# First load of a one-core decode block cut to x and the biases; its query weights join the first keys

## The chip, the core and the metric

The kernel runs on one core of a Trainium2 chip. The metric is the device time of one execution in microseconds (us); the number for a kernel is the median of several executions. A profiled execution gives a trace: every instruction on TensorE (PE for matmuls, PEld for the weight loads ahead of them), VectorE (DVE), ScalarE (ACT), GpSimd (POOL) and SyncE (SP), and every packet of the 16 DMA engines.

## What is computed

One decode step for four tokens (B = 4, model width D = 448): a layer norm, attention with 16 query heads over 8 key/value heads of width 256 on the last 1024 positions of a cache, a residual, then a layer norm twice over and an MLP with a GELU and a second residual. Cut to what matters:

```python
W = min(4096, max(256, Sk // 4))              # 1024 of 4096 positions
q = (layernorm(x) @ wq)                       # 448 -> 16 heads x 256
scores = einsum("bhqd,bhkd->bhqk", q, k[last W]) * Dh ** -0.5
o = einsum("bhqk,bhkd->bhqd", softmax(scores), v[last W])
h = x + o @ wo                                # 4096 -> 448
y = layernorm(layernorm(h))
h2 = h + gelu(y @ w1 + b1) @ w2 + b2          # 448 -> 1792 -> 448
```

All data is float32. With four tokens nearly all of the traffic is weights, keys and values, each read once.

## The kernel before

The work goes by key/value head `g` from 0 to 7. For each head the kernel projects the queries (`project_q`, matmul L214, copy to `qs` L216, transposes L222, a reduction and two copies into `qT` L225 and L229), takes the scores (`scores`, matmul `s` L237, then the maximum and the exponential), transposes the probabilities (`transpose_p`, L262), multiplies by the values (`values`, matmul `po` L276), scales and transposes the result (`heads`) and adds it to the output projection (`project_o`, `acc` L311). Queries are projected two heads ahead of their values and one ahead of their scores.

All inputs of the heads are packed on the host into eleven wide arrays, `stream0` to `stream10`, by the table `LOADS`: entry 0 holds the query weights of head 0, the keys of head 0 and the query weights of head 1 (`[("q", 0, 0), *parts("k", 0), ("q", 1, 0)]`). Each is 128 rows (one per partition) and is loaded by one DMA on SP's queue into one of three slots of the pool `ring` (tile `t`, named `stream`). A load is issued when `part` is first asked for something in it, and SP holds back the issue until all readers of the slot's earlier contents are done. So the first three loads are issued at once, and the fourth only when the first slot is free: when head 0's keys and the second query weights have been used.

The first slot is filled by two DMAs. Array `first` (L98) has 128 rows of 1828 floats: the 1792 columns of head 0's query weights (`WC`), and behind them 36 columns (`X0`) with x transposed (16), the bias b1 (16) and the bias b2 (4). Array `stream0` (L100) then brings the keys of head 0 and the query weights of head 1, 9984 columns, into the same tile.

The order of TensorE's instructions is written out by hand: the order in the program text is the order on the engine. Other engines are ordered by the framework's scheduler. At the start TensorE takes the means of x and of its squares (L193 and L194, `column_mean`), POOL the power for the reciprocal root (L208), DVE writes the normed x into `yT` (L330 to L332). Then comes `project_q` of head 0, and behind it four plus two transposes that lay out the biases and x for the end of the kernel (`pb` L348 and L349, `px` L352 and L353, copied into `rs` by ACT L350 and DVE L354). Then come the scores of head 0 and `project_q` of head 1.

After the eighth head's scores the slots are reused for the last values (`v7`, L137), the last two output weights (L383), w1 (L386) and w2 (L390, four DMAs). `keep_warm` matmuls (L361) are filler without a use for the result, at fixed places in the last third. The end is the second layer of the MLP (`second`, matmul `py` L511), a copy (L522) and two output DMAs (L525).

Of the kernel before, what the change touches and what calls it, by code (L numbers as in the profile page):

```python
# [8 lines left out]
F32 = mybir.dt.float32  # L9
# [6 lines left out]
B, D = 4, 448  # L16
HQ, HKV, SK, DH = 16, 8, 4096, 256
# [3 lines left out]
P = 128  # L21
H = P // 2
ND = 4
# [7 lines left out]
WC = 4 * D  # L31
QU = KV // 4
X0 = 2 * ND * B + 4
LOW = 3 * P
# [3 lines left out]
def parts(kind, g, quarters=range(4)):  # L38
    return [(kind, g, i) for i in quarters]


LOADS = [
    [("q", 0, 0), *parts("k", 0), ("q", 1, 0)],
    [*parts("k", 1), ("q", 2, 0), *parts("v", 0, (0, 1))],
    [*parts("v", 0, (2, 3)), ("o", 0, 0), *parts("k", 2)],
    [("q", 3, 0), *parts("v", 1), ("o", 1, 0), *parts("k", 3, (0,))],
    [*parts("k", 3, (1, 2, 3)), ("q", 4, 0), *parts("v", 2, (0, 1, 2))],
    [*parts("v", 2, (3,)), ("o", 2, 0), *parts("k", 4), ("q", 5, 0)],
    [*parts("v", 3), ("o", 3, 0), *parts("k", 5, (0, 1))],
    [*parts("k", 5, (2, 3)), ("q", 6, 0), *parts("v", 4)],  # L50
# [6 lines left out]
def width(part):  # L57
    kind, g, _ = part
    if kind in "kv":
        return QU  # L60
    return WC + {("q", 0): X0, ("q", HKV - 1): -LOW // 2}.get((kind, g), 0)


SLOT = max(sum(map(width, parts)) for parts in LOADS)
W1C = 3 * F + F // 2
C = D // 4
# [5 lines left out]
def block_kernel(ctx: ExitStack, tc, first, streams, v7, wo67, w1, w2, wq_low, out):  # L72
    nc = tc.nc
# [3 lines left out]
    once = ctx.enter_context(tc.tile_pool(name="once", bufs=1))  # L77
# [8 lines left out]
    def slot(name):  # L86
        return ring.tile([P, SLOT], F32, tag="t", name=name)

    held = {}
    streams_first = streams[0]  # L90

    def part(kind, g, i=0):
        while (kind, g, i) not in held:
            src = streams.pop(0)
            t = slot("stream")
            wanted = LOADS[len(LOADS) - len(streams) - 1]
            if src is streams_first:
                nc.sync.dma_start(t[:, : WC + X0], first)  # L98
            at = WC + X0 if src is streams_first else 0
            nc.sync.dma_start(t[:, at : at + src.shape[-1]], src)  # L100
            at = 0
            for one in wanted:
                held[one] = t[:, at : at + width(one)]
                at += width(one)
            if ("q", HKV - 1, 0) in wanted:
                held["low"] = t[:H, at : at + LOW]
                for h in range(2):
                    nc.sync.dma_start(t[h * Q : (h + 1) * Q, at : at + LOW], wq_low[h, :, : Q // 8, :])
        return held[kind, g, i]

    def wq_parts(t):
        parts = [(a, a, slice(0, 512), t[:, a * 512 : (a + 1) * 512]) for a in range(3)]
        n = t.shape[-1] - 3 * 512
        low = 512 - 2 * n
        for i in range(2):
            parts.append((3, 3 + i, slice(low + i * n, low + (i + 1) * n), t[:, 3 * 512 :]))
        if low:
            parts.append((3, 3, slice(0, low), held["low"]))
        return parts
# [4 lines left out]
    def load_k(g, h, c):  # L124
        return part("k", g, 2 * h + c).rearrange("p (b k) -> p b k", b=B)
# [5 lines left out]
    def load_v(g, c):  # L131
        return part("v", g, c).rearrange("p (c b d) -> p c b d", c=2, b=B)
# [53 lines left out]
    def spread(t):  # L186
        return t[..., ::GAP]
# [23 lines left out]
    def project_q(g, parts):  # L211
        pq = ps_m.tile([P, 512], F32, tag="m", name=f"pq{g}")
        for j, a, cols, w in parts:
            nc.tensor.matmul(pq[j * Q : (j + 1) * Q, cols], yT[: w.shape[0], a, :], w, start=True, stop=True)  # L214
        qs = once.tile([P, 512], F32, tag="qs", name=f"qs{g}")
        nc.scalar.copy(qs, pq)  # L216

        pt = ps_m.tile([P, 512], F32, tag="m", name=f"pqt{g}")
        if g == HKV - 1:
            keep_warm(3, pt)  # L220
        for i in range(2 * REP):
            nc.tensor.transpose(pt[:, i * P : (i + 1) * P], qs[:, i * P : (i + 1) * P], ident)  # L222
        q = work.tile([P, 2 * REP, B], F32, tag="q", name=f"q{g}")
        quadrants = pt.rearrange("p (i j q) -> p i q j", i=2 * REP, j=4)
        nc.vector.tensor_reduce(q, quadrants[:, :, :B, :], axis=AX.X, op=ALU.add)  # L225

        src = q.rearrange("p (r c) b -> p c b r", r=REP)
        for i in range(2):
            nc.vector.tensor_copy(qT[g % 2][:, :, :, i * REP : (i + 1) * REP], src)  # L229

    def scores(g):
        s = [ps_s.tile([P, 512], F32, tag="s", name=f"s{g}_{h}") for h in range(2)]
        mx = work.tile([P, 2], F32, tag="mx", name=f"mx{g}")
        for h in range(2):
            for c in range(2):
                for b in range(B):
                    nc.tensor.matmul(  # L237
                        s[h][b * Q : (b + 1) * Q, :], qT[g % 2][:, c, b, :], load_k(g, h, c)[:, b, :],
                        start=(c == 0), stop=(c == 1),
                    )  # L240
            nc.vector.reduce_max(mx[:, h : h + 1], s[h], axis=AX.X)  # L241
        nm = work.tile([P, 1], F32, tag="nm", name=f"nm{g}")
        nc.vector.tensor_max(nm, mx[:, 0:1], mx[:, 1:2])
        nc.vector.tensor_scalar_mul(nm, nm, -SCALE)  # L244
        p = work.tile([P, 2 * 512], F32, tag="p", name=f"p{g}")
        sums = work.tile([P, 2], F32, tag="sums", name=f"sums{g}")
        for h in range(2):
            nc.scalar.activation(  # L248
                p[:, h * 512 : (h + 1) * 512], s[h], AF.Exp, bias=nm, scale=SCALE,
                accum_out=sums[:, h : h + 1],  # L250
            )
        rec = work.tile([P, 1], F32, tag="rec", name=f"rec{g}")
        nc.vector.tensor_add(rec, sums[:, 0:1], sums[:, 1:2])
        nc.vector.reciprocal(rec, rec)
        return p, rec
# [52 lines left out]
    def project_o(g, wt):  # L308
        for i in range(4):
# [6 lines left out]
            for j in range(4):  # L316
# [3 lines left out]
                )  # L320

    t0 = part("q", 0)
    xT = t0[:, WC : WC + ND * B].rearrange("p (a b) -> p a b", a=ND)
    d = work.tile([P, ND, B], F32, tag="d", name="d_x")
    centred(d, xT, "x")
    sx = work.tile([P, ND, B], F32, tag="sx", name="sx")
# [3 lines left out]
    nc.vector.tensor_mul(yT[:, :3, :B], d[:, :3, :], rx[:, None, :].to_broadcast([P, 3, B]))  # L330
    nc.vector.tensor_mul(yT[:H, 3, :B], d[:H, 3, :], rx[:H, :])
    nc.vector.tensor_mul(yT[H:, 4, :B], d[H:, 3, :], rx[H:, :])  # L332
    project_q(0, wq_parts(t0[:, :WC]))


    b1T = t0[:, WC + ND * B : WC + 2 * ND * B].rearrange("p (c j) -> p c j", c=4)
    b2T = t0[:, WC + 2 * ND * B : WC + X0]
    nc.vector.tensor_copy(spread(zT), xT)
    b1s = work.tile([P, 2 * 512], F32, tag="p", name="b1s")
    b2s = b1s[:, 4 * P : 5 * P]  # L340
# [11 lines left out]
    nc.tensor.transpose(px[:, :P], zT.rearrange("p j q -> p (j q)"), ident)  # L352
    nc.tensor.transpose(px[:, P : 2 * P], b2s, ident)  # L353
    nc.vector.tensor_copy(rs[:, : 2 * P], px[:, : 2 * P])  # L354

    tail = []

    def keep_warm(n, to=None):
        to = tail[0][:, 0, :] if to is None else to
        for _ in range(n):  # L360
            nc.tensor.matmul(to[:Q, :512], idle[:, :Q], idle, start=True, stop=True)  # L361


    p, rec = scores(0)
    project_q(1, wq_parts(part("q", 1)))
    transpose_p(0, p)
    for g in range(HKV):
        if g + 1 < HKV:
            p, rec_next = scores(g + 1)
# [9 lines left out]
        else:  # L379
# [8 lines left out]
            at = 0  # L388
# [96 lines left out]
    for i in range(2):  # L485
        for j in range(4):
            if i <= j:
                at = PAD + C * j - P * (j - 1 + i) if j else PAD
# [34 lines left out]
    for i, queue in ((1, nc.scalar), (0, nc.sync)):  # L523
        at = i * H + LIFT
# [72 lines left out]
```

## Time and profile before

| | us |
|---|---|
| median of 3 runs | 213.75 (213.74 to 213.86) |
| the profiled execution, its own time | 213.85 |
| its span, first to last instruction | 212.1 |
| TensorE matmuls busy in the span | 147.8 (70%) |
| DVE busy | 36.8 (17%) |
| ACT busy | 24.5 (12%) |
| POOL busy | 6.2 (3%) |
| SP's DMA queue (q1), share of the 16 DMA engines | 96.9% |

The span and the time around it differ by 1.8 us, which no row covers. Busy shares are averages over the whole span. What decides is which wait ends last in each stretch, and for that the chain of waits, the DMA share by stretch and the issue times on SP are read together.

### The profile page before, as it was taken

The numbers are of one execution on the slowest core, as the hardware profiler recorded it, in microseconds if no ns is written. First come the engines' busy times: TensorE is split into PE (matmuls) and PEld (weight loads), VectorE is DVE, ScalarE is ACT, GpSimd is POOL, SyncE is SP. The second block draws the span as 40 slices with busy tenths as digits, with TensorE's granted clock in tenths as the row PEclk, the third lists the DMA queues.
The fourth block names the chain that finished last, engine by engine and source line by source line (L and its number), as shares of the span: only waits on it lengthen the run. The fifth ranks groups of instructions, "written<-read, shape, count | busy, mean of one in ns | idle before, by whom it ended". The sixth has DMA issues, their size and how long they took to land.

```text
span 212.1 us, 2553 instructions
## 1 busy us (share of the span) xinstructions
PE 147.8 (70%) x1103; PEld 57.1 (27%) x1103; DVE 36.8 (17%) x152; ACT 24.5 (12%) x58; POOL 6.2 (3%) x20
## 2 busy tenths in 40 slices
PE   0469704972891883980795780687599999999994
PEld 0333301230120520230222220131124434335443
DVE  1521400320112110220113011031022023001330
ACT  2011300030002100030003000030003002100310
POOL 6200000000000000000000000000000000000110
PEclk9999985697579599698579799589679999999999
DMA  7999898999989999998999999999999999999991
GB/s 297 414 429 510 351 501 382 449 436 419 490 365 475 407 436 442 407 490 382 457 425 425 436 425 447 401 463 409 455 414 443 389 475 387 413 426 419 427 396 61
DMA packets 3146, 88.39 MB, mean 417 GB/s; under 512 B 368, under 2 KB 576, under 8 KB 960
## 3 DMA queue, kind: packets, MB, share of 16 engines
q1 hardware_dynamic: 3120, 88.24, 96.9%
q8 instruction: 8, 0.13, 0.2%
q14 instruction: 2, 0.02, 0.0%
q10 hardware_dynamic: 16, 0.00, 0.0%
HBM read 88.23 MB, written 0.01 MB: 416 GB/s over the span
## 4 chain that ended last, share of the span: by engine, by line
DMA 70%; PE 26%; DVE 1%; SPq 1%; issue 1%; ACT 0%; ACTq 0%
DMA stream<-stream 59%; DMA w<-w 11%; PE s L237 9%; PE po L276 6%; PE wait L361 3%; PE acc L311 3%; PE ppt L262 1%; PE pq L214 1%; PE pot L301 1%; DVE o L293 0%; PE tail L361 0%; PE py L511 0%; SPq L100 0%; ACT p L248 0%; SPq L390 0%
## 5 line engine op out<-in xcount | busy, mean ns | idle before, releaser
L237 PE MATMUL s<-stream,qT 128*32 128x512 f32 x256 | 41.7, 798 | 19.3 <-DMA stream<-stream 19.3
L276 PE MATMUL po<-stream,pT 128*32 128x512 f32 x224 | 31.6, 689 | 13.3 <-DMA stream<-stream 13.3
L237 PEld LDWEIGHTS s<-stream,qT 128*32 128x32 f32 x256 | 10.8, 144 | 47.9 <-issue 35.1
L241 DVE TENSOR_REDUCE mx<-s 128x1 f32<-128x512 f32 x16 | 11.1, 691 | 63.2 <-PE s L237 63.2
L214 PE MATMUL pq<-stream,yT 128*32 128x512 f32 (+3 forms) x82 | 11.7, 635 | 7.7 <-DMA stream<-stream 4.6
L276 PEld LDWEIGHTS po<-stream,pT 128*32 128x32 f32 x224 | 7.5, 120 | 29.4 <-DMA stream<-stream 15.4
L216 ACT COPY qs<-pq 128x512 f32<-128x512 f32 x8 | 4.7, 585 | 86.8 <-PE pq L214 86.8
L293 DVE TENSOR_SCALAR o<-po,rec 128x256 f32<-128x256 f32 x8 | 3.9, 484 | 54.5 <-PE po L276 54.5
L248 ACT ACTIVATE p<-s,nm 128x512 f32<-128x512 f32 x16 | 10.9, 688 | 12.1 <-DVE nm L244 12.1
L294 ACT ACTIVATE o<-po,rec 128x256 f32<-128x256 f32 x8 | 3.8, 474 | 68.8 <-DVE o L293 68.8
L262 PE MATMUL ppt<-ident,p 128*128 128x128 f32 x64 | 11.1, 303 | 0.3
L311 PE MATMUL acc<-stream,oT 128*32 128x448 f32 x48 | 8.4, 750 | 4.2 <-DMA stream<-stream 3.0
L301 PE MATMUL pot<-ident,o 128*128 128x128 f32 x32 | 7.4, 335 | 3.8 <-DVE o L293 3.1
L222 PE MATMUL pqt<-ident,qs 128*128 128x128 f32 x32 | 6.1, 322 | 5.5 <-ACT qs L216 5.5
L214 PEld LDWEIGHTS pq<-stream,yT 128*32 128x32 f32 (+1 forms) x82 | 4.3, 127 | 16.4 <-issue 15.6
L361 PEld LDWEIGHTS <-idle 128*32 128x32 bf16 x70 | 6.2, 96 | 9.3 <-issue 3.9
L262 PEld LDWEIGHTS ppt<-ident,p 128*128 128x128 f32 x64 | 7.6, 151 | 3.7 <-ACT p L248 3.7
L361 PE MATMUL tail<-idle 128*32 128x512 bf16 x28 | 7.6, 381 | 0.0
L301 PEld LDWEIGHTS pot<-ident,o 128*128 128x128 f32 x32 | 3.6, 156 | 13.6 <-DVE o L293 10.8
L361 PE MATMUL wait<-idle 128*32 128x512 bf16 x30 | 6.8, 379 | 0.0
L222 PEld LDWEIGHTS pqt<-ident,qs 128*128 128x128 f32 x32 | 3.9, 159 | 10.4 <-ACT qs L216 8.7
L463 POOL MEMSET u<- 128x64 f32 x1 | 0.2, 151 | 175.8 <-PE hsum L410 175.8
(123 smaller groups left out, 77.3 us busy)
## 6 DMA issues: line engine op xcount, KB each, us to landing
stream<-stream SPq DMA_DIRECT2D x5, 7040.0 KB, 37.9
stream<-stream SPq DMA_DIRECT2D x2, 6912.0 KB, 41.1
stream<-stream SPq DMA_DIRECT2D x2, 4992.0 KB, 24.8
stream<-stream SPq DMA_DIRECT2D x1, 7168.0 KB, 40.3
stream<-stream SPq DMA_DIRECT2D x1, 6816.0 KB, 38.3
w<-w SPq DMA_DIRECT2D x2, 1792.0 KB, 22.3
v<-v SPq DMA_DIRECT2D x1, 3072.0 KB, 23.6
w<-wo SPq DMA_DIRECT2D x1, 1792.0 KB
```

The source lines that it names most:

```text
L214: nc.tensor.matmul(pq[j * Q : (j + 1) * Q, cols], yT[: w.shape[0], a, :], w, start=True, stop=True)
L216: nc.scalar.copy(qs, pq)
L222: nc.tensor.transpose(pt[:, i * P : (i + 1) * P], qs[:, i * P : (i + 1) * P], ident)
L237: nc.tensor.matmul(s[h][b * Q : (b + 1) * Q, :], qT[g % 2][:, c, b, :], load_k(g, h, c)[:, b, :], start=(c == 0), stop=(c == 1),)
L241: nc.vector.reduce_max(mx[:, h : h + 1], s[h], axis=AX.X)
L248: nc.scalar.activation(p[:, h * 512 : (h + 1) * 512], s[h], AF.Exp, bias=nm, scale=SCALE, accum_out=sums[:, h : h + 1],)
L262: nc.tensor.transpose(pt[:, c, :], p[:, c * P : (c + 1) * P], ident)
L276: nc.tensor.matmul(po[b * Q : (b + 1) * Q], pT[g % 2][:, c, b, :], vt[:, :, b, :], start=(c == 0), stop=(c == NKC // 2 - 1),)
L293: nc.vector.tensor_scalar_mul(o[:, :, :P], po[:, :, :P], rec)
L301: nc.tensor.transpose(pt[:, at : at + P], o[:, i, c * P : (c + 1) * P], ident)
L311: nc.tensor.matmul(acc[i * Q : (i + 1) * Q, :], oT[g % 2][:, i, :], wt[:, i, :], start=(g == 0), stop=(g == HKV - 3),)
L361: nc.tensor.matmul(to[:Q, :512], idle[:, :Q], idle, start=True, stop=True)
```

## The change

The array `first` now holds x and the biases alone, 36 columns (144 bytes a row), and goes into a tile of its own, `xs`, in a pool with one buffer. `stream0` is now all of entry 0 of `LOADS`, 11776 columns in one DMA: the query weights of head 0, the keys of head 0 and the query weights of head 1. The number of DMAs is what it was, and so is the number of bytes. In the text, `project_q` of head 0 moves behind the transposes of the biases and of x.

```diff
@@ width
-    return WC + {("q", 0): X0, ("q", HKV - 1): -LOW // 2}.get((kind, g), 0)
+    return WC - (LOW // 2 if (kind, g) == ("q", HKV - 1) else 0)
@@ block_kernel
-    streams_first = streams[0]
+    xs = once.tile([P, X0], F32, tag="xs", name="xs")
+    nc.sync.dma_start(xs, first)
@@ part
-            if src is streams_first:
-                nc.sync.dma_start(t[:, : WC + X0], first)
-            at = WC + X0 if src is streams_first else 0
-            nc.sync.dma_start(t[:, at : at + src.shape[-1]], src)
+            nc.sync.dma_start(t[:, : src.shape[-1]], src)
@@ the start
-    xT = t0[:, WC : WC + ND * B].rearrange("p (a b) -> p a b", a=ND)
+    xT = xs[:, : ND * B].rearrange("p (a b) -> p a b", a=ND)
...
-    project_q(0, wq_parts(t0[:, :WC]))
...
+    project_q(0, wq_parts(t0))
@@ kernel, on the host
-    first = np.concatenate([wq[0], xT, b1.reshape(4, 4, P).transpose(2, 1, 0).reshape(P, 16), b2], axis=1)
+    first = np.concatenate([xT, b1.reshape(4, 4, P).transpose(2, 1, 0).reshape(P, 16), b2], axis=1)
```

TensorE, from the second pair of means to the first scores, before. Here `pq_159` is head 0's query projection, `pqt_167` its transposes, `s_0_190` and `s_1_191` head 0's scores, `pq_221` head 1's query projection; `DMAHW0` counts the load of `first` and `DMAHW1` that of `stream0`:

```order
L193 MATMUL pm_sx<-sx,mean 128x12 [waits DVE_49]
L194 MATMUL pm_sx<-sx,mean 128x4
L214 MATMUL pq_159<-stream,yT 32x512 [waits DVE_49,PE_49]
L214 MATMUL pq_159<-stream,yT 32x512 x2
L214 MATMUL pq_159<-stream,yT 32x256 [waits DVE_49] x2
L222 MATMUL pqt_167<-ident,qs_165 128x128 [waits Activation_49,Pool_49]
L222 MATMUL pqt_167<-ident,qs_165 128x128 x3
L348 MATMUL pb<-ident,b1s 128x128 x3
L349 MATMUL pb<-ident,b1s 128x64
L352 MATMUL px<-ident,zT 128x128
L353 MATMUL px<-ident,b1s 128x128
L237 MATMUL s_0_190<-stream,qT_114 32x512 [waits DMAHW1_49,DVE_49,Activation_49]
```

The same place in the changed kernel (its lines are two or three lower; `pq_174`, `pqt_182` and `s_0_191` are what `pq_159`, `pqt_167` and `s_0_190` were):

```order
L191 MATMUL pm_sx<-sx,mean 128x12 [waits DVE_49]
L192 MATMUL pm_sx<-sx,mean 128x4
L345 MATMUL pb<-ident,b1s 128x128 [waits Pool_49]
L345 MATMUL pb<-ident,b1s 128x128 x2
L346 MATMUL pb<-ident,b1s 128x64
L349 MATMUL px<-ident,zT 128x128
L350 MATMUL px<-ident,b1s 128x128
L212 MATMUL pq_174<-stream,yT 32x512 [waits DMAHW1_49,DVE_49,PE_49]
L212 MATMUL pq_174<-stream,yT 32x512 x2
L212 MATMUL pq_174<-stream,yT 32x256 [waits DVE_49] x2
L220 MATMUL pqt_182<-ident,qs_180 128x128 [waits Activation_49]
L235 MATMUL s_0_191<-stream,qT_116 32x512 [waits DVE_49,PE_49]
```

The wait for the load of `stream0` (`DMAHW1`) has moved from the first scores to the first query projection, and the transposes of biases and x now stand ahead of it.

SP's queue, its first six DMAs before; the fourth `stream` is the first that has to wait for a slot:

```order
L98 DMA stream<-first 128x1828
L100 DMA stream<-stream 128x9984
L100 DMA stream<-stream 128x14080 x2
L100 DMA stream<-stream 128x13824 [waits DMAHW0_49,DMAHW1_49,DVE_49,PE_49]
L100 DMA stream<-stream 128x14080 [waits DMAHW2_49,PE_49]
```

And after:

```order
L91 DMA xs<-first 128x36
L98 DMA stream<-stream 128x11776
L98 DMA stream<-stream 128x14080 x2
L98 DMA stream<-stream 128x13824 [waits DMAHW1_49,PE_49]
L98 DMA stream<-stream 128x14080 [waits DMAHW2_49,PE_49]
```

The order of the loads stands; 1792 columns have moved from the first to the second, and the fourth load of the streams no longer waits for `first` nor for DVE, since those no longer touch its slot.

## Rows read from the trace of the kernel before

**Rows 1.** The page: the span in 40 equal slices, and bytes read.

```profile
DMA  7999898999989999998999999999999999999991
HBM read 88.23 MB, written 0.01 MB: 416 GB/s over the span
```

**Rows 2.** The chain that ended last: start us, us, what.

```profile
2.11 49.62 DMA stream<-stream
...
63.71 37.36 DMA stream<-stream
...
185.58 22.95 DMA w<-w
...
208.57 0.86 PE py L511 x24
```

**Rows 3.** Stretches: us, each engine's busy time (instructions), granted clock, DMA share, GB/s.

```profile
17.37:34.00 16.63, 7.80 (x54) 3.01 (x54) 2.88 (x12) 1.93 (x5) 0.00 (x0) 0.89 1.00 431
...
100.00:150.00 50.00, 32.74 (x208) 10.23 (x208) 7.60 (x28) 5.29 (x13) 0.00 (x0) 0.81 1.00 431
150.00:184.00 34.00, 33.11 (x223) 12.71 (x224) 5.78 (x22) 3.85 (x10) 0.00 (x0) 0.90 0.99 428
```

**Rows 4.** SP's DMA issues in order of time: start us, us, what.

```profile
0.73 0.39 SPq L98 DMA_DIRECT2D stream<-first  x1
1.18 1.74 SPq L100 DMA_DIRECT2D stream<-stream  x3
...
23.27 0.33 SPq L100 DMA_DIRECT2D stream<-stream  x1
...
184.73 2.69 SPq L390 DMA_DIRECT2D w<-w  x4
```

**Rows 5.** DMA issues of the first 2 us: count, KB each, us to landing.

```profile
stream<-stream SPq DMA_DIRECT2D x1, 4992.0 KB, 16.0
stream<-first SPq DMA_DIRECT2D x1, 914.0 KB
```

**Rows 6.** Stretches of 0.2 us at the start, columns as in rows 3.

```profile
1.40:1.60 0.20, 0.00 (x0) 0.00 (x0) 0.20 (x1) 0.20 (x1) 0.20 (x2) 1.00 0.00 0
1.60:1.80 0.20, 0.00 (x0) 0.00 (x0) 0.06 (x1) 0.20 (x1) 0.20 (x2) 1.00 1.38 219
1.80:2.00 0.20, 0.00 (x0) 0.00 (x0) 0.00 (x0) 0.20 (x1) 0.20 (x2) 1.00 0.72 110
2.00:2.20 0.20, 0.00 (x0) 0.00 (x0) 0.00 (x0) 0.01 (x1) 0.20 (x2) 1.00 0.09 37
2.20:2.40 0.20, 0.00 (x0) 0.00 (x0) 0.00 (x0) 0.00 (x0) 0.20 (x1) 1.00 0.20 73
2.40:2.60 0.20, 0.00 (x0) 0.00 (x0) 0.00 (x0) 0.00 (x0) 0.20 (x2) 1.00 1.06 329
2.60:2.80 0.20, 0.00 (x0) 0.00 (x0) 0.00 (x0) 0.00 (x0) 0.20 (x1) 1.00 0.81 292
```

**Rows 7.** Engines in order of time, 11 to 35 us: start us, us, what.

```profile
11.57 1.94 PE L214 MATMUL pq<-stream,yT 128*32 128x512 f32 x10 [3.15 <-DVE yT L331]
...
15.74 0.25 DVE L229 COPY qT<-q 128x16 f32<-128x16 f32 x2
...
17.37 4.97 PE L237 MATMUL s<-stream,qT 128*32 128x512 f32 x32 [0.36 <-DMA stream<-stream]
...
24.65 1.32 PE L262 MATMUL ppt<-ident,p 128*128 128x128 f32 x8
...
34.70 6.53 PE L237 MATMUL s<-stream,qT 128*32 128x512 f32 x32 [8.73 <-DMA stream<-stream]
```

**Rows 8.** DMA queue of 210.55 to 210.80 us: packets, MB, share of 16 engines.

```profile
q10 hardware_dynamic: 16, 0.00, 9.2%
```

**Rows 9.** TensorE at the end, in order of time.

```profile
205.73 2.41 PE L511 MATMUL py<-w,gT 128*32 128x112 f32 x88 [0.18 <-DMA w<-w]
208.57 0.82 PE L511 MATMUL py<-w,gT 128*32 128x112 f32 x24 [0.43 <-DMA w<-w]
```

More of the change, by code (lines that the diff above doesn't have):

```diff
@@ L332, in block_kernel @@
     nc.vector.tensor_mul(yT[H:, 4, :B], d[H:, 3, :], rx[H:, :])
-    project_q(0, wq_parts(t0[:, :WC]))
-    b1T = t0[:, WC + ND * B : WC + 2 * ND * B].rearrange("p (c j) -> p c j", c=4)
-    b2T = t0[:, WC + 2 * ND * B : WC + X0]
+    b1T = xs[:, ND * B : 2 * ND * B].rearrange("p (c j) -> p c j", c=4)
+    b2T = xs[:, 2 * ND * B :]
     nc.vector.tensor_copy(spread(zT), xT)
@@ L570, in part @@
         return wo[g]
-    streams = {f"stream{i}": np.concatenate([part(*one) for one in load if one != ("q", 0, 0)], axis=1) for i, load in enumerate(LOADS)}
+    streams = {f"stream{i}": np.concatenate([part(*one) for one in load], axis=1) for i, load in enumerate(LOADS)}
     w1 = packed(np.asarray(B_w1))
```

## Prediction

> **What bounds the kernel now.** I read the slices first, then the chain of waits, then the DMA share by stretch, and last the issue times on SP. In the slices the DMA row is at 9 or 8 from the second slice to the last but one [rows 1]. The chain spends most of its length in transfers, and its last steps are the transfer of w2, which lands at 185.58 + 22.95 = 208.53 us, and 24 matmuls behind it [rows 2]. The stretches tell why. Between 17 and 184 us the DMA share is 1.00, 1.00 and 0.99 at 428 to 431 GB/s, whatever TensorE does: it works 7.80 of 16.63 us in the first stretch and 33.11 of 34.00 in the last [rows 3]. So this is one long stream of bytes, and its time is when the stream starts, plus its bytes by its rate, plus what comes behind the last byte. TensorE matters only if it holds back an issue long enough for the queue to run dry, or if it is late behind the last byte.
>
> Neither is near. The fourth load of the streams is issued at 23.27 us [rows 4], but its bytes can flow only when those of the loads ahead are through, and the third landed at 2.11 + 49.62 = 51.73 us [rows 2]. The cover is some 28 us. The last big group, w2, is issued from 184.73 to 187.42 [rows 4] and lands at 208.53. Its 14 x 448 columns by 128 rows by 4 bytes are 3.21 MB, 7.5 us at 428 GB/s, so its bytes begin near 201, 13.6 us after the last of its issues. At the very end TensorE has idled 0.18 and 0.43 us for pieces of w2 [rows 9].
>
> **The change part by part.**
>
> Bytes and loads. 914 KB and 4992 KB [rows 5] become 18 KB (128 rows of 144 bytes) and 5888 KB: 5906 KB either way, in as many loads and packets, since each row is one packet before and after. At a rate that holds from the first full stretch to the last [rows 3], this term is zero.
>
> The small packets. The trace has no load of 144-byte rows. The nearest row is the output at the end: 16 packets on ACT's queue in a stretch of 0.25 us took 9.2% of 16 engines [rows 8], which is 0.092 x 16 x 0.25 / 16 = 0.023 us each; half of these carry 512 bytes and half only signal. An engine gets 8 rows, so 0.18 us, and zero is the lower end. I take zero in the sum: the next load's data comes 0.45 us later (below), and the packets lie in that gap. If the cover is gone the 0.18 us come on top, and they stand at the upper end.
> The Trainium skill, DMA: Bandwidth & Descriptors, section Specifications, says that rows under 512 bytes fall short of line rate, because the engine reads and modifies before it writes. That speaks against rows of 144 bytes. If it doubled each packet, an estimate from that page, eight would take 0.37 us and would still end inside the gap; the sum would be the same by it, and 0.37 where the cover is gone. No row here shows a load under 512 bytes a row.
>
> The start of the stream. This is the one term that is not zero. Data flows first between 1.60 and 1.80 us [rows 6], 0.87 to 1.07 us after the issue of the first load at 0.73; the second issue starts at 1.18 [rows 4], 0.45 later. Before, the 914 KB of the first load filled that gap. After, the first load is over almost at once, and the second's bytes can come from 1.18 plus 0.87 to 1.07, so from about 2.2 us. What was moved before 2.2 is small, because the engines come up slowly: 0.2 us each at 219, 110 and 37 GB/s [rows 6], 73 KB, or 0.17 us at 431 GB/s.
> How the slow part goes on decides the rest. From 2.2 to 2.8 the rows give 73, 329 and 292 GB/s, 139 KB where 431 GB/s would give 259 KB. If this slowness belongs to the clock time (the engines are up at 2.4 whatever is queued), the change loses the 0.17 us. If it belongs to the issue (each load into idle engines has its own), everything shifts by the 0.45 us between the issues. If the small load takes all of it on itself, the second runs at full rate from 2.2, wins 120 KB or 0.28 us, and the net is a gain of 0.28 - 0.17 = 0.11 us. The bounds are -0.11 and +0.45; I take +0.17, the value by the rows as they stand, which also lies at the middle of the bounds.
>
> Head 0's projection behind the big load. This moves work and adds a wait. Before, the query projection ran while `stream0` was on its way, from 11.57 us, and `qT` was ready at 15.74 + 0.25 = 15.99, 4.42 us later; the scores started at 17.37, right when the load had landed [rows 7]. After, the projection waits for the whole load. Behind it in TensorE's order stand the scores of head 0, the projection of head 1 and the transposes of the probabilities, which ended at 24.65 + 1.32 = 25.97 [rows 7]. All of these move by about 4.4 us, to 30.4. What hides this is TensorE's idle time: 8.73 us up to 34.70, when the keys of head 1 have landed [rows 7]. About 4.3 us of cover are left, and from 34.70 on the order of events is that of before. The ten matmuls, the copy, the transposes and `qT`'s copies are the same ones, so nothing is added in busy time. The transposes of the biases and of x move ahead into the time when TensorE waits for `stream0`, at no cost. On ACT the copy into `rs` now precedes that of `qs`; on DVE the copy into `rs` stands ahead of `yT`; both wait only for x and the biases, and `yT` isn't wanted until `stream0` is there.
> SP is the one that waits for TensorE here: the fourth load's issue moves from 23.27 to about 27.7, against bytes that can't flow before 51.7. If all of that cover were gone, the price would be the 4.4 us in full.
> x itself lands earlier, and the means start earlier, but the projection that uses them waits for `stream0` anyway: nothing is gained.
>
> The end. The last piece of w2 is the same 24 matmuls, the copy and the output. Zero, but for the shift of the stream.
>
> Sum: 0 + 0 + 0.17 + 0 + 0 = +0.17 us. The profiled execution was 213.85 us, a span of 212.1 and 1.8 around it; it becomes 214.02. The median of the runs lies 0.10 below the profiled one, so 213.92, rounded 213.9.
>
> **The rivals.**
>
> A second slow start (slower). The second load finds idle engines and goes through the whole slow phase of 1.6 to 2.4 us again, 0.45 us later, with the small packets not hidden: 0.45 + 0.18 = 0.63, so 214.4. For it: in 2.00 to 2.40 the engines' share falls to 0.09 and 0.20 with loads issued and waiting [rows 6], so something other than bytes was awaited. Against it: three loads are already issued by 2.92 [rows 4], and the share is 1.06 from 2.4 on [rows 6]. It decides from the point where the second load's data starts after about 2.6 us.
>
> The small load shows the fixed price of a load (slower). If the stream can't start until the small load is complete, its whole latency stands in the open. The nearest row for a load with little data is none, so the bound is from the first load of before: data from 1.7, and 914 KB at 431 GB/s (2.2 us) end near 3.9, while the chain has the streams moving without a break from 2.11 [rows 2]. A stream that starts at 3.7 instead of 2.2 costs 1.5 us: 215.4. Against it: nothing on SP waits between the first three issues [rows 4], and the share at the later change from load to load stays at 1.00 [rows 3].
> The Trainium skill, DMA: Bandwidth & Descriptors, section Anatomy of one DMA, puts a fixed 2.0 us on each load beside its bytes (fitted to loads that GpSimd issues); by that rule the time would be this rival's, 1.5 us more. The unbroken share of 1.00 speaks against a price paid in the queue.
>
> TensorE loses its cover (slower). The 4.4 us reach an issue that matters. It would take a cover smaller than that, and the smallest found is 13.6 us. Price up to 4.4 us, 218 at worst.
>
> The slowest engine gains (faster). A load lands when the slowest of the 16 engines is done. `stream0` was usable at 17.37 [rows 7]; 6.05 MB at 431 GB/s are 14.03 us, so the slowest engine ran as if it had begun at 3.3, 1.1 us after the 2.2 of the change. Part of this is the way from the last byte to the signal, which stays. If half of it is slow start that the small load takes on itself, the gain is 0.55 us: 213.2.
>
> **How the numbers follow.** A measurement of this kernel can tell about 0.2%, 0.43 us, from no change. Forecast (within 213.3 and 214.2, 213.9 likeliest): 0.66. Second slow start, 214.4: 0.15. Fixed price, 215.4: 0.03. Lost cover: 0.04. Slowest engine, 213.2: 0.12. So faster 0.12, same 0.66, slower 0.22. For the range, the bounds of the start, -0.11 and +0.45, with the 0.18 of the small packets above, give 213.6 to 214.4; below it reaches toward the faster rival, to 213.3, which leaves out under 2 in 10.
>
> **What would show it.** Right: in the changed profile the first packets again come at 1.6 to 1.8, the stream's full rate from about 2.4 to 2.8, `stream0` lands near 17.5, head 0's projection starts there and its scores 4.4 us later, head 1's scores start on their load near 34.9, the fourth load is issued near 28, the DMA share stays at 1.00 in the middle stretches, and w2 lands near 208.7. Wrong: a stretch of DMA share well under 1 after 3 us, a landing of `stream0` later than 17.9 or earlier than 17.0, TensorE still at head 0 at 35 us, or an end that moves by more than the start did.

## The result, and the profile after

The changed kernel takes 214.53 us (median of 6 runs), the kernel before 213.80 beside it: a ratio of 1.0035, interval 1.0024 to 1.0046, so 0.5 to 1.0 us slower. The forecast was 213.9 with a range up to 214.4. The profiled execution after took 214.41 us, 0.56 more than the one before; its span is 212.6. So the medians put the loss at 0.73 us and the two traces at 0.56.

The chain that ended last, after (start us, us, what), answers to [rows 2]:

```profile
63.91 38.05 DMA stream<-stream
...
185.91 23.16 DMA w<-w
209.11 0.85 PE py L510 x23
```

w2 lands at 185.91 + 23.16 = 209.07 us instead of 208.53, 0.54 later, and the matmuls behind it take what they took. So the loss is already there when the last byte comes. The stretches, columns as in [rows 3]:

```profile
17.37:34.00 16.63, 11.66 (x68) 4.54 (x68) 3.27 (x14) 2.52 (x6) 0.00 (x0) 0.99 1.01 437
...
100.00:150.00 50.00, 31.81 (x208) 10.11 (x208) 7.60 (x28) 5.29 (x13) 0.00 (x0) 0.83 0.99 429
150.00:184.00 34.00, 32.34 (x219) 13.24 (x223) 5.77 (x21) 3.85 (x10) 0.00 (x0) 0.90 0.98 423
```

The DMA share in the middle is again 0.98 to 1.01: the engines don't run dry there, so the loss isn't there. TensorE at the start, after (start us, us, what, idle ahead of it and who ended it), answers to [rows 7]:

```profile
2.80 0.57 PE L191 MATMUL pm_x<-xs,mean 128*128 128x12 f32 x2 [2.80 <-DMA xs<-first]
...
17.95 1.94 PE L212 MATMUL pq<-stream,yT 128*32 128x512 f32 x10 [10.30 <-DMA stream<-stream]
...
22.47 5.78 PE L235 MATMUL s<-stream,qT 128*32 128x512 f32 x32 [0.70 <-DVE qT L227]
...
30.56 1.32 PE L260 MATMUL ppt<-ident,p 128*128 128x128 f32 x8
34.59 6.11 PE L235 MATMUL s<-stream,qT 128*32 128x512 f32 x28 [2.71 <-DMA stream<-stream]
```

x is there at 2.80 instead of some 5.5 us. The first stream lands at 17.95 instead of 17.37, 0.58 later: all that the end is late by is there already behind the first load. Head 0's scores start 4.52 us behind its landing, and TensorE is done at 31.88 with 2.71 us left before the keys of head 1.

What happened at the start is seen in two views. First the stretches, after, as in [rows 6]:

```profile
1.60:1.80 0.20, 0.00 (x0) 0.00 (x0) 0.06 (x1) 0.20 (x1) 0.20 (x2) 1.00 0.08 14
1.80:2.00 0.20, 0.00 (x0) 0.00 (x0) 0.00 (x0) 0.20 (x1) 0.20 (x2) 1.00 0.48 63
2.00:2.20 0.20, 0.00 (x0) 0.00 (x0) 0.00 (x0) 0.01 (x1) 0.20 (x2) 1.00 0.16 12
2.20:2.40 0.20, 0.00 (x0) 0.00 (x0) 0.00 (x0) 0.00 (x0) 0.20 (x1) 1.00 8.06 2359
```

A packet counts here, whole, where it starts, so 2359 GB/s and a share of 8 are rows of 47 KB that start in this stretch: ten rows (2359 x 0.2 are 472 KB), which took 8.06 x 16 x 0.2 = 25.8 us together, 2.58 us each. At the rate of the middle, 431 GB/s over 16 engines, such a row takes 1.75 us. The 18 KB of the small load trickle through between 1.6 and 2.2 (0.2 us each at 14, 63 and 12 GB/s), and the stream's first rows start from 2.2, as the issue 0.45 us later says. Second, the queue's packets that start in the first 16 us: packets, MB, and their time as a share of 16 engines. Before:

```profile
q1 hardware_dynamic: 272, 6.05, 90.2%
```

After:

```profile
q1 hardware_dynamic: 272, 6.05, 93.0%
```

The same packets and the same bytes (the first load and the first stream, whole) took 2.8% of 16 us longer on an engine, 0.45 us. The engines didn't only start later, they also took longer over their first rows. Before, too, some of that is paid: at the rate of the middle, 6.05 MB at 431 GB/s are 14.04 us, and 90.2% of 16 are 14.43. The first nine rows there, 1.60 to 2.00 in [rows 6], took 0.75 us each where 7.3 KB take 0.27.

Adding up the starts, ends and sizes of the single packets in the two traces separates the two parts. Up to 20 us an engine stood idle for 2.07 us on average before and for 2.27 after: 0.20 us of later start. Its rows took 0.44 us more before, and 0.88 after, than the same bytes take from 20 to 100 us: 0.44 us of slower rows. The sum, 0.64 us, is still 0.62 at 185 us.

### The profile page after: what moved, and what is told of

Read it like the earlier page. It is cut to its first block, busy times and chain, and to the rows that moved or that the text cites. A ratio compares the mean times of both kernels' runs of the same rounds, so it can differ in the third digit from the quotient of the medians.

```text
span 212.6 us, 2551 instructions
## 1 busy us (share of the span) xinstructions
PE 148.2 (70%) x1103; PEld 57.8 (27%) x1103; DVE 37.4 (18%) x152; ACT 24.5 (12%) x58; POOL 6.3 (3%) x20
## 4 chain that ended last, share of the span: by engine, by line
DMA 62%; PE 30%; another core or an unknown queue 3%; DVE 1%; SPq 1%; issue 1%; ACT 1%; ACTq 0%
DMA stream<-stream 52%; PE s L235 11%; DMA w<-w 11%; PE po L274 7%; PE wait L360 3%; PE acc L309 3%; PE ppt L260 2%; PE pq L212 2%; PE pot L299 1%; PE pqt L220 1%; DVE o L291 0%; PE tail L360 0%; PE py L510 0%; ACT p L246 0%
## 5 line engine op out<-in xcount | busy, mean ns | idle before, releaser
L235 PE MATMUL s<-stream,qT 128*32 128x512 f32 x256 | 42.2, 805 | 14.2 <-DMA stream<-stream 13.5
L223 DVE TENSOR_REDUCE q<-pqt 128x16 f32<-128x64 f32 x8 | 1.8, 224 | 26.5 <-PE pqt L220 26.5
```

Source lines behind the costliest of these rows:

```text
L235: nc.tensor.matmul(s[h][b * Q : (b + 1) * Q, :], qT[g % 2][:, c, b, :], load_k(g, h, c)[:, b, :], start=(c == 0), stop=(c == 1),)
```

## The experiments

The start theory: the stream of loads begins late, and everything behind it moves by that. The TensorE theory: head 0's projection behind the big load holds something back. Each time below is a median beside runs of the kernel before on the same chip (213.67 to 213.71 us); the intervals are of the ratio to it.

**Another load in x's company (e1_swap).** The first load keeps its 1828 columns, but with head 1's query weights; those of head 0 come with the keys, and TensorE's order is that of the changed kernel.

```diff
-    [("q", 0, 0), *parts("k", 0), ("q", 1, 0)],
+    [("q", 1, 0), ("q", 0, 0), *parts("k", 0)],
...
+    project_q(0, wq_parts(part("q", 0)))
     tail = []
```

> The first load is as large as in the kernel before (1828 columns), but carries the query weights of head 1 with x and the biases; those of head 0 come with the first keys, so head 0's projection waits for that load as in the changed kernel. Start theory (the stream of loads begins late because the small first load leaves the DMA engines idle and the second load then starts slowly): the start is that of before, so 213.8 us. TensorE theory (head 0's projection behind the big load holds something back): 214.5, as the changed kernel. The second load lands near 17.4 us by the first theory, and the fourth stream is issued near 28.5 by both.

213.66 us, ratio 0.9999 (0.9990 to 1.0008). TensorE in this run:

```profile
17.39 1.93 PE L214 MATMUL pq<-stream,yT 128*32 128x512 f32 x10 [7.13 <-DMA stream<-stream]
...
21.90 6.09 PE L237 MATMUL s<-stream,qT 128*32 128x512 f32 x32 [0.70 <-DVE qT L229]
...
34.04 5.14 PE L237 MATMUL s<-stream,qT 128*32 128x512 f32 x32 [2.41 <-DMA stream<-stream]
```

Head 0's projection waits for the load, the scores start 4.5 us after it, just as in the changed kernel, and the time is that of before. The TensorE theory has fallen. What differs from the changed kernel is the first load: its size, and the place of x in the first slot, which the next run tests.

**The tile of x (e5b_fill0).** The changed loads, with x in the first slot as before (`N0` is 0).

```diff
-    xs = once.tile([P, X0], F32, tag="xs", name="xs")
-    nc.sync.dma_start(xs, first)
...
+                nc.sync.dma_start(t[:, : N0 + X0], first)
+            at = N0 + X0 if src is streams_first else 0
```

> The changed kernel with x and the biases in the first slot instead of a tile of their own; loads, sizes and TensorE's order are those of the changed kernel. Start theory: the tile does not matter, 0.65 to 0.8 us above before. Rival (the separate tile, which takes one wait off the fourth stream's issue and moves addresses): as before.

214.48 us, 1.0036 (1.0023 to 1.0049). The loss is as large with x in the first slot, so the tile is not it; the sizes of the loads are enough.

**Two small loads ahead (e4_two).**

```diff
-    nc.sync.dma_start(xs, first)
+    nc.sync.dma_start(xs[:, : ND * B], first[:, : ND * B])
+    nc.sync.dma_start(xs[:, ND * B :], first[:, ND * B :])
```

> The changed kernel with the suspected cost doubled: x and the biases come in two small loads ahead of the first stream, so that it is issued another 0.45 us later. Start theory: 0.45 us more than the changed kernel, 215.0 us, the first stream lands near 18.4. TensorE theory: 214.5, no change, since TensorE waits for the same load in the same order.

215.07 us, 1.0061 (1.0049 to 1.0074). SP, TensorE and the end of the chain:

```profile
0.73 0.39 SPq L91 DMA_DIRECT2D xs<-first  x1
1.19 0.41 SPq L92 DMA_DIRECT2D xs<-first  x1
1.64 28.10 SPq L99 DMA_DIRECT2D stream<-stream  x4
```

```profile
18.48 1.94 PE L213 MATMUL pq<-stream,yT 128*32 128x512 f32 x10 [11.19 <-DMA stream<-stream]
```

```profile
186.11 23.36 DMA w<-w
```

The stream's issue moves by another 0.45 us (1.18 to 1.64), its first load lands 0.53 later than in the changed kernel, w2 0.40 later, and the time is 0.54 more by the two medians (0.67 with each taken against the kernel before beside it). An issue that carries next to nothing costs about its own 0.45 us here, and the end of the kernel follows.

**The gap filled (e5_fill512).** 512 columns of the query weights (`N0`) travel with x: 274 KB, in the slot as before.

```diff
-                nc.sync.dma_start(t[:, : WC + X0], first)
+                nc.sync.dma_start(t[:, : N0 + X0], first)
```

> The changed kernel, but the first load carries x, the biases and the first 512 columns of head 0's query weights (548 columns, 274 KB, 0.65 us at 431 GB/s), so that the gap of 0.45 us between the two issues is covered by data. Start theory where only the gap counts: 213.8 to 214.0. Start theory where the first packets of the long rows are slow whatever lies ahead: 214.2 to 214.4. TensorE theory: 214.5, since head 0's projection still ends only behind the second load.

213.89 us, 1.0010 (1.0001 to 1.0019). The first stream is usable at 17.35 us. Most of the loss is gone, as the theory had it where only the gap counts: 0.22 us are left of 0.73. The packets of the first 16 us:

```profile
q1 hardware_dynamic: 272, 6.05, 91.4%
```

That is 1.2% of 16 us above before, 0.19 us.

**Gap kept, first rows short (e6_three), and the same loads in another order (e9_between).** Both cut the first stream behind head 0's query weights. In the first the order is x, query weights, rest; in the second, whose diff this is, the query weights are issued first and x second.

```diff
-    nc.sync.dma_start(xs, first)
...
-            nc.sync.dma_start(t[:, : src.shape[-1]], src)
...
+                nc.sync.dma_start(t[:, :WC], src[:, :WC])
+                nc.sync.dma_start(xs, first)
+                nc.sync.dma_start(t[:, WC:n], src[:, WC:])
```

> The changed kernel with its first stream split in two loads: head 0's query weights (rows of 7168 bytes, as long as the first load's before) and behind them the rest. The gap of 0.45 us behind the small load stays. Theory gap alone: as the changed kernel, 0.7 us above before, the keys land near 17.9. Theory gap and long first rows (the first rows after an idle start are slow, and the more so the longer they are; in the run with x on ScalarE's queue, which has no gap, 0.47 us were lost): 0.35 to 0.5 us above before, the keys land near 17.7.

> The same three loads as in the run with the first stream split (x and the biases; head 0's query weights with rows of 7168 bytes; the rest), but the query weights are issued first and the small load second, so that the stream starts with the first issue and 0.94 MB cover the small load. Gap theory: 213.6 to 213.9, as before, the keys land near 17.4. Rival (a small load of its own costs 0.6 to 0.8 us wherever it stands, or a third load does): 214.3 to 214.6.

214.57 us, 1.0036 (1.0023 to 1.0049), and 214.07, 1.0017 (1.0008 to 1.0026). Head 0's scores wait for the keys until 17.78 in the first and 17.59 in the second:

```profile
17.78 5.17 PE L237 MATMUL s<-stream,qT 128*32 128x512 f32 x32 [4.72 <-DMA stream<-stream]
```

```profile
17.59 5.81 PE L240 MATMUL s<-stream,qT 128*32 128x512 f32 x32 [1.62 <-DMA stream<-stream]
```

Swapping two issues gives 0.50 us back by the medians, 0.30 between the profiled executions. The packets say which part that is: up to 20 us an engine was idle for 2.25 us in the first run and 1.88 in the second, and its rows were slow by 0.72 and 0.75. The order that leaves the engines without bytes costs the gap. But neither came out as expected. The first did not gain by its short rows, and the second kept 0.37 us without a gap.

**One more load (e10_split, e10b_later).** The kernel before with one load cut in two: the second of the kernel, whose diff this is, or the fourth.

```diff
+            for a, b in ((0, KV), (KV, n)) if src is streams_first else ((0, n),):
+                nc.sync.dma_start(t[:, at + a : at + b], src[:, a:b])
```

> The kernel before with its second load (head 0's keys and head 1's query weights) cut in two at the same bytes: three loads at the start, first rows of 7.3 KB, no small load, no gap. Theory that one more load near the start has a price: 0.2 to 0.4 us above before, as in the run with the small load between two others. Theory that only the gap and long first rows cost: as before, 213.6 to 213.8, and then the 0.37 us of that run belong to the small load itself.

> The kernel before with its fourth load (the third stream, 7040 KB) cut in two at the same bytes: one more load, but its issue and first rows lie behind 13 MB that are already queued. Theory that a load has a price wherever it stands: 0.2 to 0.4 us above before. Theory that only the start of the stream counts: as before, 213.6 to 213.8.

213.94 us, 1.0010 (1.0001 to 1.0019), and 213.90, 1.0009 (0.9999 to 1.0018). So one more load may cost about 0.2 us, at the start or later; the intervals reach zero or nearly so. It would account for about half of what the run with x in the middle kept, and it would hide a gain of the short rows in the run before it. The changed kernel has as many loads as before, so this price is no part of its loss.

**Long first rows without a gap (e3_behind, e2_act, e8b_quarter, e8_long).** Two runs issue the first stream first, with x behind it on SP or beside it on ScalarE's queue; two add a quarter or three quarters of the first keys to the first load of the kernel before, so that its rows are 15.5 or 31.9 KB (`N1`), and have head 0's projection at the changed kernel's place. The three edits of the diff are those of the run on SP, of the run on ScalarE's queue and of the two others.

```diff
+                nc.sync.dma_start(t[:, : src.shape[-1]], src)
+                nc.sync.dma_start(xs, first)
...
-    nc.sync.dma_start(xs, first)
+    nc.scalar.dma_start(xs, first)
...
-                nc.sync.dma_start(t[:, : WC + X0], first)
+                nc.sync.dma_start(t[:, : WC + X0 + N1], first)
```

> The changed kernel with the first stream issued first and x and the biases behind it on the same queue. No gap, first rows of 47 KB, x lands only with the first stream, near 17.4 us, so that TensorE starts 6 us later than in the changed kernel. Gap alone: as before, 213.7. Gap and long first rows: 0.3 to 0.5 us above before, as on ScalarE's queue. TensorE's lateness as a cost: 214.5 or more.

> The changed kernel, but the small load of x and the biases is issued on ScalarE's DMA queue, so that the first stream is the first issue on SP, 0.45 us earlier. Start theory: 213.7 to 214.0, the first stream lands near 17.4 instead of 17.9. TensorE theory: 214.5, since TensorE's order is unchanged.

> The kernel before with one quarter of head 0's keys added to its first load, so first rows of 15.5 KB between the 7.3 KB of before and the 31.9 KB of the run with three quarters, which lost 0.70 us; no gap. Theory of long first rows: 0.2 to 0.5 us above before. Gap alone: as before, and then the 0.70 us come from something else in that run, such as x landing late.

> The kernel before with three quarters of head 0's keys added to its first load, so rows of 31.9 KB instead of 7.3 KB, no gap ahead of the second load, and head 0's projection in the changed kernel's place. x lands some 7 us later, still in time for the projection. Theory gap alone: as before, within 0.1 us. Theory gap and long first rows: 0.15 to 0.4 us above before, the second load lands 0.15 to 0.3 us later than 17.37.

| run | first rows | time | ratio |
|---|---|---|---|
| stream first, x behind (e3_behind) | 47 KB | 214.13 | 1.0021 (1.0012 to 1.0030) |
| x on ScalarE's queue (e2_act) | 47 KB | 214.14 | 1.0020 (1.0011 to 1.0029) |
| a quarter of the keys added (e8b_quarter) | 15.5 KB | 214.01 | 1.0013 (1.0004 to 1.0022) |
| three quarters added (e8_long) | 31.9 KB | 214.40 | 1.0033 (1.0020 to 1.0046) |

All four have no gap ahead of their stream, no more loads than before, and lose 0.3 to 0.7 us. In the second and the third row x lands at 17.84 and 8.51 us, and they lose 0.47 and 0.31 us, so x's lateness isn't what they have in common. The packets of the first 16 us in the run with a quarter of the keys added:

```profile
q1 hardware_dynamic: 271, 6.02, 92.0%
```

One row of the second load less than before has started, and still the packets took 1.8% of 16 us more, 0.29 us, close to the 0.31 us of the run. So first rows longer than 7.3 KB go with a slower start. The rows that start in the first 0.4 to 0.7 us of these traces took longer than their bytes take at 431 GB/s by 0.71 us each at 15.5 KB, 0.85 at 31.9 KB and 0.81 at 47 KB (x behind), against 0.48 at 7.3 KB in the kernel before. But the run that filled the gap lost 0.19 us of packet time with first rows of 2.2 KB, and the sum of idle time and slow rows at 20 us is only 0.1 to 0.3 us above before in all four runs, less than their times lost. Three quarters added stand out: 0.2 us behind before at 20 us and again at 205 us, yet w2's last row ends 0.80 us later. So most of that run's 0.70 us is not in its average engine. Packets carry no engine's name in these traces; why the first rows are slow, and what the rest of the four losses is, is not settled.

**Two queues (e7_two_queues).** x on SP as in the changed kernel, the first stream at the same moment on ScalarE's queue, the others on SP.

```diff
-            nc.sync.dma_start(t[:, : src.shape[-1]], src)
+            queue = nc.scalar if ("q", 0, 0) in wanted else nc.sync
+            queue.dma_start(t[:, : src.shape[-1]], src)
```

> The changed kernel with its first stream issued on ScalarE's queue at the same time as the small load on SP, so that the gap between the two is gone while x still comes first and alone; the second stream on SP now starts 0.45 us after the first on another queue. Gap theory: 0 to 0.3 us above before, the first stream lands near 17.5. Rival: the two queues share the engines row by row, the first stream lands late, near 25 to 30, and the time is 1 us or more above before.

214.31 us, 1.0032 (1.0020 to 1.0044). No gap, but no repair either:

```profile
11.05 0.57 PE L192 MATMUL pm_x<-xs,mean 128*128 128x12 f32 x2 [11.05 <-DMA xs<-first]
...
26.32 1.94 PE L213 MATMUL pq<-stream,yT 128*32 128x512 f32 x10 [10.42 <-DMA stream<-stream]
```

The first stream lands at 26.32, since it shares the engines with the second one on SP. The rival had the landing right, but its price of 1 us or more did not come: 0.61 us are lost.

No version beat the kernel before; the best, the swap of the query weights, equals it.

## Why the prediction was wrong

**What bounds the kernel: right.** The time is the start of the stream plus its bytes. The first stream's landing moved by 0.58, the landing of w2 by 0.54, and the DMA share between stayed at 0.98 to 1.01. In three of the kernels head 0's projection starts when the first stream lands, and the times follow that landing: 17.39, 17.95 and 18.48 us go with 213.66, 214.53 and 215.07. The run with the gap filled departs from this by 0.2 us: 17.35 and 213.89.

**Head 0's projection: right.** 4.4 us of delay and 4.3 of cover were forecast; 4.5 us and 2.71 of cover were found, and the fourth load went out at 29.18 instead of 27.7, 23 us early enough:

```profile
29.18 0.33 SPq L98 DMA_DIRECT2D stream<-stream  x1
```

The cover came out 1.6 us smaller, of which 0.81 is that the scores took 5.78 us instead of 4.97, and 0.58 that the first stream landed later. The swap run, with 2.41 us of cover, shows the price: none.

**The small packets: right.** They pass between 1.6 and 2.2, inside the gap.

**The start of the stream: the step that failed.** The term was +0.17 us, with +0.45 as its upper end; it measured 0.58 at the landing of the first stream and 0.73 in the time. The prediction's own sign of being wrong, a landing later than 17.9, is there at 17.95. The choice between "belongs to the clock time" and "belongs to the issue" went the wrong way: engines that had been through 18 KB were no readier for the stream than idle ones. Their first long rows took 2.58 us each; in the run with x behind the stream, where the engines came from idle, the 13 rows that start by 2.0 us took 2.56. Beyond the choice, the bounds were too narrow. They counted bytes not moved before 2.2 us, and took the rows that follow at their usual time. The rows of the stream themselves took 0.45 us longer per engine for the same bytes (93.0% against 90.2%), which neither end held. Packet by packet the trace splits the loss into 0.20 us of later start and 0.44 of slower rows. The later start is less than the 0.45 us between the issues, since the kernel before had idle engines then too: nine rows had started by 2.0 us, on 16 engines. The runs agree in size: the gap is worth 0.3 to 0.5 us where two issues were swapped, and long first rows without a gap cost 0.3 to 0.5 us with the same number of loads (0.7 in one). Why a first row is slow stays open.

[rows 6] held the sign, and it was misread. A packet counts there where it starts, so the low shares of 2.00 to 2.40 are not engines that all wait: most of the nine rows that started before 2.00, at 0.75 us each, were still running. What they show is rows at well over twice their usual time, and the bytes counted before 2.2 were not all moved by then.

**The rivals.** "A second slow start", at 214.4 us with a chance of 0.15, is nearest to what happened. Its number, +0.63, is close partly by luck: it added the whole 0.45 us between the issues and 0.18 of small packets, where the later start was 0.20, the small packets lay in the gap, and the rows were slower than those of before. Its condition (the second load's data after about 2.6 us) did not come, since the first rows started from 2.2 and were slow from there. It should have counted as the likelier case, since no row shows that a load is spared the slow start because another came first. "The fixed price of a load", 215.4, did not come: a whole further small load ahead of the stream added 0.54 us. The 3.7 us from which that rival counts follow from none of its rows. The Trainium skill, DMA: Bandwidth & Descriptors, section Anatomy of one DMA, has 2.0 us for a load that GpSimd issues; as a price that the queue pays ahead of the next load, the measured 0.54 speaks against it, and the page itself puts most of the 2.0 us on completion. "The slowest engine gains" had the sign wrong: the first stream landed later.

## What to carry to other kernels

Where a kernel is one unbroken stream of loads, its first issue should carry at least as many bytes as the engines move until the second issue's data can come (here 0.45 us, some 190 KB). In this kernel what was lost at the start, 0.64 us at 20 us, was still lost at 185. That many bytes were not quite enough: a first load of 274 KB was still 0.2 us slower than the 914 KB of before. A small input was best packed with the first large one; a load ahead of it that carried next to nothing cost about its issue time. Price a start from idle by the time that the first rows took, not by the bytes alone, and before reading a short stretch ask whether it counts a packet where it starts or while it runs.

## What was not expected of the hardware

A small load beside a stream on another queue lands late. x and the biases, 18 KB, landed at 2.80 us with nothing beside them. On ScalarE's queue beside the first stream they landed at 17.84:

```profile
17.84 0.57 PE L191 MATMUL pm_x<-xs,mean 128*128 128x12 f32 x2 [17.84 <-DMA xs<-first]
```

Of its 128 rows, 112 had started by 16 us, so one for each engine, on average, was still to come:

```profile
q10 hardware_dynamic: 112, 0.02, 0.6%
```

On SP, with the stream on ScalarE's queue, they landed at 11.05. An engine has eight rows of each load (128 rows, 16 engines); at eight long rows of 1.7 us each (6.03 MB at 431 GB/s are 14.0 us in all), taking turns row by row would hold the last small row back until nearly the end of the stream. The Trainium skill, DMA: Bandwidth & Descriptors, section Queues, rings and completion order, says that an engine takes turns between the queues it has work for, packet by packet, with 9 to 17 descriptors in a typical packet. The two landings agree with the turns; in this trace each row is a packet of its own, and a turn is one row.

One more load in the same stream of bytes measured 0.2 us, at the start and behind 13 MB of queued loads alike (1.0010 and 1.0009), at the edge of what these runs can tell. No row shows where it would be spent: the DMA share of the kernel before holds 0.99 to 1.00 across the changes from load to load [rows 3].
